# A two-layer channel network in two phases: seven block products for all four batches, hidden rows by way of DRAM

## The chip, the cores and the metric

One core of one Trainium2 chip runs the kernel. TensorE (PE) multiplies, VectorE (DVE) and ScalarE (ACT) do the elementwise work, GpSimd (POOL) and SyncE (SP) issue DMAs beside the other engines. The metric is the device time of one execution in microseconds, as the median of several.

## The reference

Four batches of 448 tokens by 768 channels go through three stages; the last is the one that changes.

```python
attn = 1 / (1 + exp(-(q @ k.T / 8 - log(448))))        # 4 batches, 12 heads, 448 x 64
x = (attn @ v), heads side by side                     # 448 x 768 per batch
k = maximum(xk @ w_k, 0); v = k * k @ w_v              # 768 -> 1024 -> 768, xk and xr mix x
x = v / (1 + exp(-(xr @ w_r)))                         # with the token before it
u = x + real(fft2(x))
un = (u - mean(u)) / sqrt(var(u) + 1e-6)               # over the 768 channels
out = u + maximum(un @ w_ch1, 0) @ w_ch2               # 768 -> 3072 -> 768
```

The weights arrive eight bytes wide and are made fp32 on the chip.

## The kernel before

A large fp32 product is made of three fp32r matmuls: both operands are split into a high part (a cast on ScalarE) and a low part (a subtraction on VectorE), and high by high, high by low and low by high are summed in PSUM. A matmul has 128 rows of weight and a moving operand of 448 columns, one batch. The helper class Order holds a planner: generators for every piece of work ask for keys (`need`), emit instructions, and its clock decides in which order each engine's queue is written. Every matmul is recorded at line 202, VectorE's two-operand work at 237 and 245, ScalarE's copies and casts at 254 and activations at 256, DMAs at 261 (POOL, accumulating) and 263. The order of a queue is fixed at build time; an instruction that must wait holds up what stands behind it on its engine.

The program runs attention, the mix (`keys`, `receptance`, `values`), and, batch by batch beside `values`, the transform: `spectrum` and `mixed` make u in `x2_t[b]` (x_0 to x_3 in the rows), `centre` and `scale` (from line 1015) subtract the mean and make rs, one over the standard deviation. In the transform, pa and qa are first-step matmuls whose split parts are called pq, and a second set of matmuls of 226 columns is recorded under pq too.

The network (`network`, line 1412) has 3072 hidden channels in 12 groups of 256. Batches 0 and 1 go through plain products: `ffn1` (36 matmuls for each 256 hidden channels and batch), `hidden` (relu and the split of h on chip), `ffn2` (36 matmuls as well), whose results `out_done` adds into `acc`, loaded from u. `convert` makes w_ch1 and w_ch2 fp32, stores them and keeps their split parts for the plain products. Batches 2 and 3, called the second pair, then go through a block form in which a 2 x 2 block product takes seven products of sums of blocks instead of eight. `PRODUCTS` lists layer one: A blocks and sums S of the weights (`second_weights` makes them, 9 matmuls a product, `pair1` with 63 a group), B blocks and sums T of the rows (`prepare_rows`, from c_d in DRAM, multiplied by rs there). `SECOND` does the same for layer two in pairs of groups (`second_weights2`, `second_rows`, `second`, `second_done`, 126 matmuls a pair of groups) for NS = 5 pairs. Each result is copied by ScalarE into a stage tile and added into DRAM by accumulating DMAs of POOL. The sixth pair of groups takes plain `ffn2` (144 matmuls), and its results with those in DRAM make the output of batches 2 and 3.

## Time and profile before

| | |
|---|---|
| median of three runs | 1159.62 us (1159.06 to 1161.45) |
| the profiled execution | 1159.6 us, its span 1157.8 us |
| TensorE busy | 1148.8 us, 99% of the span |
| VectorE, ScalarE busy | 773.2 us (67%), 602.5 us (52%) |
| DMA | 243.52 MB, 210 GB/s on average |

The time lies 1.8 us over the span, which runs from the first to the last instruction. A busy share is an average over stages; what an engine is worth in one stage is read from the windows and the timeline there. A matmul's record starts at its issue and ends when its last result is out, so records of neighbours overlap, and the distance from one start to the next (the pitch) is what a row of them costs.

### The profile page before, as it was taken

The numbers are of one execution on the slowest core, as the hardware profiler recorded it, in microseconds if no ns is written. First come the engines' busy times: TensorE is split into PE (matmuls) and PEld (weight loads), VectorE is DVE, ScalarE is ACT, GpSimd is POOL, SyncE is SP. The second block draws the span as 40 slices with busy tenths as digits, with TensorE's granted clock in tenths as the row PEclk, the third lists the DMA queues.
The fourth block names the chain that finished last, engine by engine and source line by source line (L and its number), as shares of the span: only waits on it lengthen the run. The fifth ranks groups of instructions, "written<-read, shape, count | busy, mean of one in ns | idle before, by whom it ended". The sixth has DMA issues, their size and how long they took to land.

```text
span 1157.8 us, 16560 instructions
## 1 busy us (share of the span) xinstructions
PE 1148.8 (99%) x6094; PEld 1009.1 (87%) x6094; DVE 773.2 (67%) x1293; ACT 602.5 (52%) x1091; POOL 106.7 (9%) x154
## 2 busy tenths in 40 slices
PE   8999999999999999999999999999999999999998
PEld 3576766799999999999999999999999999999998
DVE  3867757576514679898766666665477777877762
ACT  6887887667520133244544444443137567665740
POOL 0000001000000000000000000000003243442420
PEclk9999999999999999999999999999999999999999
DMA  7765789568949355476675656563917696977994
GB/s 242 241 221 210 260 311 349 227 232 290 332 141 292 109 198 192 147 283 262 212 248 193 229 196 227 199 220 112 354 40 177 126 202 110 192 136 163 181 191 167
DMA packets 92549, 243.52 MB, mean 210 GB/s; under 512 B 10610, under 2 KB 46516, under 8 KB 92340
## 3 DMA queue, kind: packets, MB, share of 16 engines
q1 hardware_dynamic: 74596, 204.70, 50.9%
q0 software_dynamic: 17584, 37.30, 17.1%
q8 instruction: 48, 0.79, 0.3%
q10 hardware_dynamic: 288, 0.46, 0.1%
q14 instruction: 33, 0.27, 0.1%
HBM read 145.45 MB, written 99.04 MB: 211 GB/s over the span
## 4 chain that ended last, share of the span: by engine, by line
PE 96%; ACT 1%; DMA 1%; DVE 0%; issue 0%; SPq 0%; DVEq 0%
PE f L202 32%; PE m L202 10%; PE v L202 10%; PE k L202 9%; PE r L202 7%; PE av L202 6%; PE sc L202 4%; PE f_W L202 4%; PE f_X L202 3%; PE f_Z L202 3%; PE f_Y L202 2%; PE pq L202 1%; DMA w<-w_d 1%; PE sc_c L202 1%; PE pa L202 1%; PE qa L202 1%
## 5 line engine op out<-in xcount | busy, mean ns | idle before, releaser
L202 PE MATMUL f<-un,w1h 128*128 128x448 f32 x576 | 164.2, 364 | 0.0
L202 PE MATMUL f<-h,w2h 128*128 128x448 f32 x576 | 163.2, 363 | 0.0
L237 DVE TENSOR_TENSOR acc<-acc,f 128x448 f32<-128x448 f32 x126 | 77.3, 618 | 79.7 <-PE f L202 79.2
L261 POOL DMA_DIRECT2D u_d<-stage x75 | 64.7, 931 | 602.9 <-ACT stage L254 595.6
L202 PEld LDWEIGHTS f<-un,w1h 128*128 128x128 f32 x576 | 108.0, 188 | 7.6 <-issue 0.6
L202 PEld LDWEIGHTS f<-h,w2h 128*128 128x128 f32 x576 | 108.1, 188 | 7.0
L202 PE MATMUL v<-k,wvh 128*128 128x448 f32 x384 | 111.9, 365 | 0.0
L202 PE MATMUL f<-un,w1l 128*128 128x448 f32 x288 | 103.9, 361 | 0.0
L202 PE MATMUL f<-h,w2l 128*128 128x448 f32 x288 | 103.7, 360 | 0.0
L202 PE MATMUL m<-hs,sw_h 128*128 128x448 f32 x324 | 91.5, 363 | 0.0
L256 ACT ACTIVATE sg<-sc,bias_s 128x448 f32<-128x448 f32 x144 | 78.3, 650 | 12.9 <-PE sc L202 12.8
L202 PEld LDWEIGHTS v<-k,wvh 128*128 128x128 f32 x384 | 72.0, 188 | 4.9 <-issue 0.6
L202 PE MATMUL k<-xkh,wkh 128*128 128x448 f32 x192 | 70.6, 368 | 0.9 <-ACT kt L256 0.9
L202 PE MATMUL k<-xkl,wkh 128*128 128x448 f32 x192 | 70.2, 366 | 0.0
L202 PE MATMUL k<-xkh,wkl 128*128 128x448 f32 x192 | 70.2, 366 | 0.0
L202 PE MATMUL v<-k,wvl 128*128 128x448 f32 x192 | 69.7, 363 | 0.0
L254 ACT COPY stage<-m 128x448 f32<-128x448 f32 x105 | 55.7, 534 | 16.8 <-PE m L202 7.0
L202 PEld LDWEIGHTS m<-hs,sw_h 128*128 128x128 f32 x324 | 60.8, 188 | 4.0
L256 ACT ACTIVATE h<-f 128x448 fp32r<-128x448 f32 x48 | 26.1, 544 | 71.3 <-PE f L202 71.3
L202 PE MATMUL m<-hs,sw_l 128*128 128x448 f32 x162 | 58.3, 360 | 0.0
L202 PEld LDWEIGHTS f<-un,w1l 128*128 128x128 f32 x288 | 53.9, 187 | 3.9 <-issue 0.2
L202 PE MATMUL av<-sg,v 128*64 128x448 f32 x288 | 57.2, 544 | 0.0
(227 smaller groups left out, 2502.1 us busy)
## 6 DMA issues: line engine op xcount, KB each, us to landing
w_raw<-in_w SPq DMA_DIRECT2D x40, 768.0 KB, 4.8
u_d<-stage POOLq DMA_DIRECT2D x75, 224.0 KB, 5.9
w_d<-w_bits SPq DMA_DIRECT2D x40, 384.0 KB, 2.6
k_d<-kp SPq DMA_DIRECT2D x32, 448.0 KB, 3.2
k<-k_d SPq DMA_DIRECT2D x32, 448.0 KB, 5.9
a<-w_d SPq DMA_DIRECT2D x24, 384.0 KB, 5.4
w<-w_d SPq DMA_DIRECT2D x24, 384.0 KB, 10.6
v<-in_v SPq DMA_DIRECT2D x24, 256.0 KB, 3.5
```

The costliest lines, as they stand in the source:

```text
L202: self.nc.tensor.matmul(out, lhs, rhs, start=start, stop=stop, skip_group_check=skip)
L237: eng.tensor_tensor(out, a, c, op=op)
L254: self.nc.scalar.copy(out, a)
L256: self.nc.scalar.activation(out, a, fn, **kw)
L261: self.nc.gpsimd.dma_start(out, src, accum_op=ALU.add)
```

## The change

All four batches go through the block form, as pair 0 (batches 0 and 1) and pair 1 (2 and 3), and the network has two phases.

In phase one only layer one runs. The first PL = 4 groups of pair 0 are still plain (8 chunks of 128 hidden channels, `plain`, 18 matmuls a chunk and batch). Then come 15 visits: groups 4 to 6 for pair 0, groups 7 to 11 for both pairs with the same weight sums, and groups 0 to 6 for pair 1. A visit is 63 matmuls a pair. The seven products are ordered anew and use three PSUM banks a pair; a copy of the first product, the seed, starts the second bank chain. The relu results go to DRAM unsplit (`put`, h_d). `rows0` and `rows1` make the operands of the pairs; the rows of pair 1 stay on chip and are worked on 1344 wide, and the results of batches 1 to 3 need no way through c_d. w_ch2 is converted in halves in phase one (`convert_rest`), its seven pieces and sums (`combine`) go to DRAM (v_d).

In phase two `second` takes one pair after the other: seven products, each over six steps (`tp`) of two groups and 18 matmuls. A product's 36 matmuls for one result are summed in one PSUM bank, three results beside each other; products 0 and 2, 1 and 3, 4 and 6 share a chain. `second_splits` loads the weight piece (w, 768 wide) and the hidden rows (r, 896 wide) of a step, subtracts rows where a T is asked for, and splits both (sw, hs). Results are added on VectorE into tiles loaded from u and stored to the output; no accumulating DMA is left. `convert` for the plain products, `ffn2`, `master`, `second_done` and the way of rs through DRAM are gone; their lines are left out below.

```diff
+PL, JO, EARLY = 4, 7, 8
...
 PRODUCTS = (
     ("A11", "B11", "X"),
+    ("S3", "T3", "W"),
     ("S2", "T2", "Y"),
-    ("S3", "T3", "Z"),
+    ("A12", "B21", "X"),
+    ("S1", "T1", "Y"),
+    ("A22", "T4", "W"),
+    ("S4", "B22", "Y"),
+)
+SECOND = (
+    ("A11", "B11", "X"),
     ("S1", "T1", "W"),
     ("A12", "B21", "X"),
+    ("S4", "B22", "W"),
+    ("S3", "T3", "Z"),
+    ("S2", "T2", "Y"),
     ("A22", "T4", "Z"),
-    ("S4", "B22", "W"),
 )
-LATE = ("T1", "B21", "T4", "B22")
-SECOND = (("A11", "B11"), ("S1", "T1"), ("A12", "B21"), ("S4", "B22"), ("S2", "T2"), ("S3", "T3"), ("A22", "T4"))
-NS = NG // 2 - 1
+PIECE = {nm: i for i, (nm, _, _) in enumerate(SECOND)}
+VISITS = [(g, (0,)) for g in range(PL, JO)] + [(g, (0, 1)) for g in range(JO, NG)] + [(g, (1,)) for g in range(JO)]
+LAST0 = 7 * (NG - PL) - 1
+CHUNKS = FF2 // 128
...
-            if b > 1:
-                o.at["c_d", b, i] = o.dma(c_d[b][:, 2 * i : 2 * i + 2], xx) + 2.0
             if b > 0 and i == 0:
-        if b > 1:
-            yield from o.need(("c_d", b, 2))
-            o.at["centre", b] = o.now
-            yield from scale(b)
-            return
         yield from scale(b)
         rs = rs_t[b]
         for i in range(KD):
             t = o.tt(V, u[:, i], u[:, i], rs, ALU.mult)
             yield t
-            if i % 2:
+            o.at["norm", b, i] = t
+            if i % 2 and b < 1:
                 o.at["c_d", b, i // 2] = o.dma(c_d[b][:, i - 1 : i + 1], u[:, i - 1 : i + 1]) + 2.0
-        yield from o.need(("c_d", b, 2))
+        if b < 1:
+            yield from o.need(("c_d", b, 2))
         o.at["centre", b] = o.now
...
+        yield from o.need(("centre", 2))
+        yield from split("B11", *new("B11"), b11)
+        yield from split("B21", *new("B21"), b21)
+        yield from o.need(("centre", 3), ("rows", 0))
+        v = x2_t[3]
+        b12, b22 = v[:, 0:3], v[:, 3:6]
+        o.dma(t_d[1], b22)
+        yield o.tt(V, b11, b12, b11, ALU.subtract)
+        t1 = np_.tile([128, 2, 3, S], F32R, tag="x2", name="T1_1", bufs=3)
+        yield from split("T1", t1[:, 0], t1[:, 1], b11)
+        yield o.tt(V, b12, b22, b12, ALU.subtract)
+        yield from split("T3", *new("T3"), b12)
+        yield o.tt(V, b12, b22, b11, ALU.subtract)
+        yield from split("T2", *new("T2"), b12)
+        yield o.tt(V, b21, b21, b12, ALU.subtract)
+        yield o.dma(t_d[0], b21) + 2.0
+        for i, nm in enumerate(("T4", "B22")):
+            t = np_.tile([128, 2, 3, S], F32R, tag="x2", name=f"{nm}_1", bufs=3)
+            yield o.dma(t[:, 1].bitcast(F32), t_d[i]) + 0.5
+            yield from split(nm, t[:, 0], t[:, 1], t[:, 1].bitcast(F32))
+        shift(tp1, "tp1")
+        o.at["rows", 1] = o.now
+    wt_t, place_t = {}, {}
+    for v, (g, ps) in enumerate(VISITS):
+        for j in range(2):
+            i = 2 * (v - NG + PL) + j
+            place_t[v, j] = ("w0", "w1", "k0", "k1", "k2")[i % 5] if i >= 0 else f"w{j}"
+    def visit_loads():
+        last = {}
+        for v, (g, _) in enumerate(VISITS):
...
+        def visit(v):
+            g, ps = VISITS[v]
+            bk, tm = {}, {}
+            def after(n, p):
+                x, y, w = (bk[k, p][:, 0:S] if (k, p) in bk else None for k in "XYW")
+                    bk["Y", p] = bank(f"f1_{v}_{p}_Y")
+                    o.at["seed", v, p] = o.act(bk["Y", p][:, 0:S], x)
+                    o.at["w7", v, p] = o.act(tmp("w7", p), w)
+                    o.at["u2", v, p] = o.act(tmp("u2", p), y)
+                    yield from put(p, 0, g, stage(p, 0, g), x)
+                    o.at["c22", v, p] = t = o.tt(V, tm["w7", p], tm["w7", p], y, ALU.add)
+                    yield t
+                    yield from put(p, 3, g, tm["w7", p], tm["w7", p])
+                    yield o.tt(V, tm["u2", p], tm["u2", p], w, ALU.add)
+                    yield from put(p, 2, g, tm["u2", p], tm["u2", p])
+                    yield from put(p, 1, g, stage(p, 1, g), y)
...
+            def step(n, p, i, lhs, rhs, k):
+                if i == 0 and n < 2:
+                    bk[k, p] = bank2(f"f1_{v}_{p}_{k}")
+                o.mm(bk[k, p][:, 0:S], lhs, rhs, i == 0 and n < 2, i == 8, skip=True)
...
-        order = [(ffn1, "w1", (0, 0)), (ffn1, "w1", (1, 0)), (ffn2, "w2", (0, 0))]
-        order += [(ffn1, "w1", (0, 1)), (ffn1, "w1", (1, 1)), (ffn2, "w2", (0, 1)), (ffn2, "w2", (1, 0))]
-        order += [(ffn1, "w1", (2, 0)), (ffn2, "w2", (1, 1)), (ffn1, "w1", (2, 1))]
-        for g in range(2, NG, 2):
-            order += [(ffn1, "w1", (g, 0)), (ffn1, "w1", (g, 1))] if g > 2 else []
-            order += [(ffn2, "w2", (g, 0))]
-            order += [(ffn1, "w1", (g + 1, 0)), (ffn1, "w1", (g + 1, 1)), (ffn2, "w2", (g + 1, 0)), (ffn2, "w2", (g + 1, 1))]
-        order += [(pair1, "p1", (0, 3)), (pair1, "p1", (1, 3))]
-        for p in range(NS):
-            order += [(second, "s2", (p, range(5))), (pair1, "p1", (2 * p + 2, 3))]
-            order += [(second, "s2", (p, (5, 6))), (pair1, "p1", (2 * p + 3, 3))]
-        order += [(ffn2, "v2", (NG - 1, 2)), (ffn2, "v2", (NG - 1, 3))]
...
+        def second(p):
+            def after(m, e, ps):
...
+                if m == 0:
+                    if e == 0:
+                        tiles("t")
+                    o.at["tc", p, e] = o.act(out[p, "t"][:, e], ps)
+                elif m == 1:
+                    if e == 0:
+                        tiles("22", "11")
+                    yield from o.need(("res", p, "22"))
+                    o.at["v", p, e] = add("22", e, ps)
+                elif m == 2:
+                    yield from store("11", e, add("11", e, ps))
+                elif m == 3:
+                    if e == 0:
+                        tiles("12", "21")
+                    yield from o.need(("res", p, "12"))
+                    o.at["w", p, e] = add("12", e, ps)
+                elif m == 4:
+                    o.at["z", p, e] = add("22", e, ps)
+                elif m == 5:
+                    t = out[p, "t"][:, e]
+                    yield o.tt(V, t, t, ps, ALU.add)
+                    t1, t2 = add("12", e, t), add("22", e, t)
+                    o.at["y", p, e] = add("21", e, t)
+                    yield from store("12", e, t1)
+                    yield from store("22", e, t2)
+                else:
+                    yield from store("21", e, add("21", e, ps))
+                yield o.now
+            def step(m, e, i, j, lhs, rhs):
+                first = {2: 0, 3: 1, 6: 4}.get(m, m)
+                if i == 0 and first == m:
+                    chain[p, m, e] = (bank2 if m in (0, 4) else bank)(f"m_{p}_{m}_{e}")
+                ps = chain[p, first, e][:, 0:S]
+                o.mm(ps, lhs, rhs, i == 0 and first == m, i == 35, skip=True)
+                if i == 35:
...
+            for m in range(7):
+                for tp in range(NG // 2):
+                    j = 42 * p + 6 * m + tp
+                    for t in range(2):
+                        for e in range(3):
+                            es = slice(128 * e, 128 * e + 128)
+                            for i, (a, c) in enumerate(((0, 0), (0, 1), (1, 0))):
+                                o.feed.append(partial(step, m, e, 6 * tp + 3 * t + i, j, sw[:, a, t, es], hs[:, c, t]))
...
+        for b in range(2):
+            pss = ([], [])
+            for t in (0, 3):
+                for f in range(2):
+                    yield from plain(f, b, range(t, t + 3), pss[f])
+        for f in range(2, 2 * PL):
+            for b in range(2):
+                yield from plain(f, b)
+        for v in range(len(VISITS)):
+            yield from visit(v)
+        for p in range(2):
+            yield from second(p)
...
+        for j in range(total):
+            p, m, tp = j // 42, j % 42 // 6, j % 6
+            if j > 1:
+                yield from o.need("right")
+            if j > 3:
+                yield from o.need(("pair", j - 4))
+            w, t = raw.pop(j)
+            yield t
+            sw_t[j] = from_pool(j, "sw", [128, 2, 2, n], F32R, f"sw_{j}")
+            yield o.act(sw_t[j][:, 0], w)
+            o.spawn(low(("sw", j), sw_t[j], w))
+            nm = SECOND[m][1]
+            q = {"B11": (0,), "T1": (1, 0), "B21": (2,), "B22": (3,), "T3": (3, 1), "T2": (3, 0), "T4": (2, 3)}[nm]
+            for x in q:
+            r = [r_t[p, x, tp] for x in q]
+            dst = r[{"T1": 1, "T3": 1}.get(nm, 0)]
+            if len(q) > 1:
+                yield o.tt(V, dst, r[0], r[1], ALU.subtract)
+            hs_t[j] = from_pool(j, "hs", [128, 2, 2, S], F32R, f"hs_{j}")
+            yield o.act(hs_t[j][:, 0], dst)
+            o.spawn(low(("hs", j), hs_t[j], dst))
...
+        if (f % 2, h) == (1, 1):
+            store("A22", w)
+            pc["S1"] = piece(f"s1_{g}")
+            yield from combine("S1", pc["S1"], pc[0, 1], w, ALU.add)
+        elif (f % 2, h) == (0, 0):
+            store("A11", w)
+            pc["S2"] = piece(f"s2_{g}")
+            yield from combine("S2", pc["S2"], pc["S1"], w, ALU.subtract)
+            yield from combine("S3", pc[0, 1], w, pc[0, 1], ALU.subtract)
+        elif (f % 2, h) == (1, 0):
+            store("A12", w)
+            yield from combine("S4", piece(f"s4_{g}"), w, pc["S2"], ALU.subtract)
...
+        yield from convert(wst, "raw", 3, 3, todo1, room, ready)
+        yield from o.need(("rows", 1))
+        yield from convert(wst, "raw", 3, 3, todo2, room, ready, None, 3.5)
+        yield o.now + 4.0
+        o.at["converted"] = o.now
```

By count, layer one and two together have 3258 matmuls of 448 columns before and 3060 now.

The first place is VectorE in the transform of batch 3, between the addition that ends block 3 of x_3 and the low parts of qa. xl and yl are low parts of the transform's operands, evod, xf and yf its folded rows, h the hidden part of a plain product. Before:

```order
L237 TENSOR_TENSOR xl_5288<-xf_5278,xh_5287 128x2x225
L245 SCALAR_TENSOR_TENSOR h_0_0_5354<-f_0_0_0_5313,h_0_0_5354 128x448
L237 TENSOR_TENSOR yl_5290<-yf_5279,yh_5289 128x2x223
L237 TENSOR_TENSOR evod_5189<-x_3_4853 128x448 x2
L237 TENSOR_TENSOR xf_5278<-evod_5189 128x223
L895 COPY xf_5278<-evod_5189 128x2
L237 TENSOR_TENSOR yf_5279<-evod_5189 128x223
L237 TENSOR_TENSOR x_2_4377<-x_2_4377,mean_5365 128x448 x2
L245 SCALAR_TENSOR_TENSOR h_0_1_5393<-f_0_0_1_5351,h_0_1_5393 128x448
L237 TENSOR_TENSOR xl_5288<-xf_5278,xh_5287 128x225
L237 TENSOR_TENSOR xf_5278<-evod_5189 1x223
L904 COPY xf_5278<-evod_5189 1x2
```

Now, with un_1 the low parts of batch 1's normalized rows, x_1 times rs their source, and s and blk the first weight sums of the visits:

```order
L248 TENSOR_TENSOR sum_u_5373<-sum_u_5373,x_2_4477 128x448 x2
L248 TENSOR_TENSOR x_3_4986<-v_5_5379,rv_5_5326 128x448
L248 TENSOR_TENSOR x_1_4072<-x_1_4072,rs_5259 128x448
L248 TENSOR_TENSOR un_1_5473<-x_1_4072,un_1_5473 128x448
L248 TENSOR_TENSOR xl_5427<-xf_5417,xh_5426 128x2x225
L248 TENSOR_TENSOR yl_5429<-yf_5418,yh_5428 128x2x223
L248 TENSOR_TENSOR sum_u_5373<-sum_u_5373,x_2_4477 128x448 x2
L248 TENSOR_TENSOR s_0_5506<-a_1_5469 128x384
L248 TENSOR_TENSOR blk_5507<-a_0_5465,blk_5507 128x384
L248 TENSOR_TENSOR evod_5358<-x_3_4986 128x448 x2
L248 TENSOR_TENSOR xf_5417<-evod_5358 128x223
L915 COPY xf_5417<-evod_5358 128x2
```

The two hidden parts have gone, and the scaling and the low parts of un_1, sums of x_2 and weight sums have come between the same folds.

The second place is VectorE where the rows of pair 1 are made. Before, acc_6321 is the tile in which four 448-wide row blocks are combined, among the sums and splits of plain products for batch 0:

```order
L237 TENSOR_TENSOR acc_5367<-acc_5367,f_6_0_2_7123 128x448
L237 TENSOR_TENSOR acc_6321<-acc_6321 128x448
L237 TENSOR_TENSOR acc_5367<-acc_5367,f_6_0_3_7132 128x448
L237 TENSOR_TENSOR w2l_1_7048<-w_7_1_bits,w2h_1_7047 128x768
L237 TENSOR_TENSOR acc_5367<-acc_5367,f_6_0_4_7147 128x448
L237 TENSOR_TENSOR T_1_7160<-acc_6321,T_1_7160 128x448
L237 TENSOR_TENSOR acc_5367<-acc_5367,f_6_0_5_7156 128x448
```

Now this is the start of the visits, from a sum of visit 0 (w_0) to the low part of the second product of visit 1 (blk_6407):

```order
L248 TENSOR_TENSOR w_0_6294<-w_0_6294,f_0_0_Y 128x448
L248 TENSOR_TENSOR T_1_6352<-x_2_4477,T_1_6352 128x1344
L248 TENSOR_TENSOR u_0_6318<-u_0_6318,f_0_0_W 128x448
L248 TENSOR_TENSOR s_1_6358<-a_1_6315 128x384
L248 TENSOR_TENSOR blk_6359<-a_0_6290,blk_6359 128x384
L256 SCALAR_TENSOR_TENSOR w_23_1_6363<-w_23_raw_6298,w_23_1_6363 128x384
L248 TENSOR_TENSOR x_3_4986<-x_3_4986 128x1344
L248 TENSOR_TENSOR a_1_6315<-a_0_6290,a_1_6315 128x384
L248 TENSOR_TENSOR T_1_6405<-x_3_4986,T_1_6405 128x1344
L248 TENSOR_TENSOR a_0_6290<-s_1_6358,a_0_6290 128x384
L248 TENSOR_TENSOR blk_6407<-a_1_6315,blk_6407 128x384
```

A row operation is now three blocks wide, and three such instructions stand ahead of a low part of the very next product.

The third place is VectorE in layer two. Before, in the middle of a pair of groups:

```order
L237 TENSOR_TENSOR a_1_9362<-a_0_9360,a_1_9362 128x384
L237 TENSOR_TENSOR hs_0_9421<-rows,hs_0_9421 128x448
L237 TENSOR_TENSOR a_0_9360<-s_5_9400,a_0_9360 128x384
L237 TENSOR_TENSOR hs_1_9422<-rows,hs_1_9422 128x448
L237 TENSOR_TENSOR sw_l<-w_2_9249,sw_h 128x768
L237 TENSOR_TENSOR rows<-rows 128x896
L237 TENSOR_TENSOR blk_9418<-a_0_9360,blk_9418 128x384
```

Now, in the last product of pair 0 (T4, a difference of rows):

```order
L248 TENSOR_TENSOR r_3_2_9057<-r_3_2_9057,r_0_2_8066 128x896
L248 TENSOR_TENSOR sw_9764<-w_9675,sw_9764 128x768
L248 TENSOR_TENSOR out_0_9272<-out_0_9272,m_4_0_9627 128x448
L248 TENSOR_TENSOR out_0_9272<-out_0_9272,m_4_1_9631 128x448
L248 TENSOR_TENSOR out_0_9272<-out_0_9272,m_4_2_9635 128x448
L248 TENSOR_TENSOR hs_9782<-r_3_2_9057,hs_9782 128x896
L248 TENSOR_TENSOR r_3_3_9069<-r_3_3_9069,r_0_3_8911 128x896
L248 TENSOR_TENSOR sw_9797<-w_9703,sw_9797 128x768
```

The weight sums (blk, a, s) of layer one have left this place; a step now has one subtraction of rows, one low part of weights and one of rows, and the three sums of a finished product stand between them.

## Rows read from the trace of the kernel before

**Rows 1.** The page, busy time and share of the span by engine

```profile
PE 1148.8 (99%) x6094; PEld 1009.1 (87%) x6094; DVE 773.2 (67%) x1293; ACT 602.5 (52%) x1091; POOL 106.7 (9%) x154
```

**Rows 2.** The span and TensorE's mean granted clock, by core

```profile
core 0: 1157.8 us, clock 1.000
```

**Rows 3.** Waits of TensorE: what it waited for, us in all, times, longest

```profile
PE sc L202 <- DMA q<-in_q: 3.8, 1, 3.8
PE k L202 <- ACT kt L256: 0.9, 3, 0.5
PE f_W L202 <- DVE u L237: 0.4, 1, 0.4
```

**Rows 4.** Groups by line and shape, TensorE: busy us, mean ns of one

```profile
L202 PE MATMUL f<-un,w1h 128*128 128x448 f32 x576 | 164.2, 364 | 0.0
...
L202 PE MATMUL m<-hs,sw_h 128*128 128x448 f32 x324 | 91.5, 363 | 0.0
```

**Rows 5.** Timeline, TensorE in layer two: start, us, operation, count

```profile
719.70 0.36 PE L202 MATMUL f<-h,w2l 128*128 128x448 f32 x1
...
720.30 0.36 PE L202 MATMUL f<-h,w2l 128*128 128x448 f32 x1
...
723.90 0.36 PE L202 MATMUL f<-h,w2l 128*128 128x448 f32 x1
```

**Rows 6.** Timeline, VectorE: back to back instructions of four widths

```profile
905.11 0.55 DVE L237 TENSOR_TENSOR s<-a 128x384 f32<-128x384 f32 x1
905.58 0.62 DVE L237 TENSOR_TENSOR extra<-rows,extra 128x448 fp32r<-128x448 f32 x1
906.12 0.55 DVE L237 TENSOR_TENSOR a<-a,a 128x384 f32<-128x384 f32 x1
...
908.46 1.09 DVE L237 TENSOR_TENSOR rows<-rows 128x896 f32<-128x896 f32 x1
909.46 0.95 DVE L237 TENSOR_TENSOR w<-w 128x768 f32<-128x768 f32 x1
910.33 0.55 DVE L237 TENSOR_TENSOR blk<-a,blk 128x384 fp32r<-128x384 f32 x1
```

**Rows 7.** Timeline, VectorE in the transform of batch 3

```profile
484.13 0.62 DVE L237 TENSOR_TENSOR x<-v,rv 128x448 f32<-128x448 f32 x1
...
508.98 0.56 DVE L237 TENSOR_TENSOR pq<-qa,pq 111x384 fp32r<-111x384 f32 x1 [0.60 <-ACT pq L254]
```

**Rows 8.** Busy time of each engine in that stretch

```profile
487.40:509.00 21.60, 21.60 (x132) 20.10 (x131) 19.71 (x44) 8.93 (x18) 0.00 (x0) 1.00 0.95 346
```

**Rows 9.** Timeline, ScalarE: casts and a copy of three widths

```profile
879.53 0.84 ACT L254 CAST sw_h<-w 128x768 fp32r<-128x768 f32 x1
880.27 0.54 ACT L254 COPY stage<-m 128x448 f32<-128x448 f32 x1
880.69 0.53 ACT L254 CAST blk<-a 128x384 fp32r<-128x384 f32 x1
```

**Rows 10.** DMA of the fullest 20 us of the network

```profile
DMA packets 2893, 7.31 MB, mean 365 GB/s; under 512 B 325, under 2 KB 1318, under 8 KB 2892
```

**Rows 11.** The page, DMA issues: count, KB each, us to landing

```profile
w_raw<-in_w SPq DMA_DIRECT2D x40, 768.0 KB, 4.8
u_d<-stage POOLq DMA_DIRECT2D x75, 224.0 KB, 5.9
...
a<-w_d SPq DMA_DIRECT2D x24, 384.0 KB, 5.4
```

**Rows 12.** Timeline, the end of the span

```profile
1152.26 2.73 SPq L263 DMA_DIRECT2D out<-acc  x2
...
1153.61 0.36 PE L202 MATMUL f<-h,v_l 128*128 128x448 f32 x1
1154.01 0.62 DVE L237 TENSOR_TENSOR acc<-acc,f 128x448 f32<-128x448 f32 x1 [1.78 <-PE f L202]
```

**Rows 13.** Busy time and granted clock just after the first wait

```profile
3.80:8.00 4.20, 4.16 (x16) 1.88 (x19) 0.17 (x1) 1.93 (x4) 0.00 (x0) 1.00 0.94 272
```

836 lines of the change are left out of this document (394 added, 442 removed).

## The prediction

> **What bounds the kernel now.** I read the page first, then the clock, TensorE's waits, its groups, and only then single stretches. TensorE is busy for 1148.8 of 1157.8 us [rows 1] at a granted clock of 1.000 [rows 2], and its waits come to 5.1 us, of which 3.8 are the first load [rows 3]. VectorE is busy for 67% and ScalarE for 52% [rows 1]; nobody waits for them. So the time now is the list of matmuls times their pitch, and every matmul less is time gained, as long as the helpers stay hidden. The second question is therefore how near each helper is to showing, stretch by stretch.
>
> The duration of one matmul, 363 or 364 ns [rows 4], is not its price, since matmuls overlap. In the timeline 21 of them start between 719.70 and 723.90 [rows 5]: 4.20 / 21 = 0.200 us. The same holds for VectorE: one 448-wide sum lasts 0.62 us, but the next starts 0.54 behind it; 384 wide 0.47, 896 wide 1.00, 768 wide 0.87 [rows 6]. From 448 to 896 is 0.46 more, so 1344 wide is 1.46 by the same slope. On ScalarE a 768 cast is 0.74, a 448 copy 0.42 [rows 9].
>
> **What is removed.** Before, layer one of batches 0 and 1 is 2 x 24 x 18 = 864 matmuls and their layer two another 864; batches 2 and 3 take 12 x 63 = 756 and 5 x 126 = 630, and 144 for their last group pair: 3258. After: 2 x 8 x 18 = 288 plain ones, 20 block products of a pair and group, 20 x 63 = 1260, and 2 x 42 x 18 = 1512: 3060. All have 448 columns, and the rest of TensorE's list is the same. 198 x 0.200 = **39.6 us less**. The 0.4 us wait of f_W for u [rows 3] goes with its pattern. The 75 accumulating stores of 224 KB [rows 11] go too, at nothing: TensorE never waited for them. If every new step hid as well, the time would be 1159.6 - 39.6 - 0.4 = 1119.6. The profiled execution took 1159.6 with a span of 1157.8, and the median of the runs is 1159.62, so no correction is due.
>
> **What is added, and where it shows.** I went along VectorE's queue between two points at which it meets TensorE, summed pitches, and set that against TensorE's work between the same points.
>
> (a) The transform of batch 3. From x of column block 3 to the second pq low part VectorE has 49 instructions before, whose pitches sum to 22.2 us; they took from 484.13 to 509.54, 25.4 us [rows 7]. In 21.6 us of this it was busy for 19.71 while TensorE never paused [rows 8]: already over nine tenths full, 1.9 us of waiting, and 23.5 / 22.2 = 1.06 times the pitches for dependent and PSUM operands. After, the same stretch holds 88: 45 of 448 wide (24.1), 24 of about 224 at 0.30 by the slope (7.2), 9 of 384 or 390 (4.2), 7 of about 448 (3.8) and three tiny ones, 39.5 us. The new ones are the scaling of x_1, the low parts of un_1 and T_0, and the work on x_2, which used to stand later or went by way of DRAM. TensorE has 129 full matmuls (25.8 us), 83 of 192 to 226 columns (7.7 in proportion) and one of the mean, some 35 us. With 0.4 us from a last matmul to VectorE's start [rows 12]: 39.5 x 1.06 + 0.4 - 35 = 7.3. The ends are 4.9 (bare pitches) and 10.4 (1.14, the 25.4 with its waits). VectorE is the late one here, so ScalarE's waits mostly vanish: I take **7.3**.
>
> By the Trainium skill (VectorE: DVE Perf Modes, section "The TRN2 errata — SBUF-src ops pay a fixed extra latency per instruction") an fp32 sum costs (N + 151) / 0.96 ns, 0.624 us for 448, and the fixed part is exposed between instructions. The trace agrees with it for one instruction, 0.62, and not for a row of them, 0.54 [rows 6]. By the page the stretch would be an estimated 47 us and this term 12.
>
> (b) The rows of pair 1. Between the sum of visit 0's fifth product and the low part that visit 1's second product needs, VectorE now has three 1344-wide instructions (4.4), a 448 sum and seven of 384 (3.3), 8.3 us with the first sum, where TensorE has 29 matmuls, 5.8. Before, the same rows came one 448 block at a time, with ffn products around them. 8.3 + 0.4 - 5.8 = 2.9; the third 1344 instruction also waits for a cast of some 1.2 us on ScalarE (by the slope of [rows 9]), of which 0.5 is covered: **3.7**, ends 2 and 5.
>
> (c) The visits of pair 1 alone. One is 63 matmuls, 12.6 us. In the four densest SP issues some 21.8 MB (weights twice 384 KB per visit, halves of w_ch2 in, seven pieces out, hidden rows out, first rows of layer two in): 21.8 MB / 50.4 us = 430 GB/s, where the fullest 20 us of the trace moved 365 [rows 10]. 21.8 MB at 365 is 59.7 us: the queue falls 9 us behind and later catches up. Three raw buffers and five weight places take up about half. A late raw half is worse than its own delay: ScalarE meets it in order, and the casts and seed copies behind it are what TensorE waits for. I take **4**, ends 0 and 12.
>
> (d) The start of layer two: its first weight load is issued at the phase's end, lands in some 3 to 5 us (5.4 for 384 KB [rows 11]), and then a cast of 0.74 and a low part of 0.87 [rows 6, 9] stand before TensorE, which has two pairs made up ahead, 7.2 us: **1**, ends 0 and 2.
>
> (e) Layer two. A step of 18 matmuls is 3.6 us; VectorE needs 0.87 + 1.00, and one sum of 1.00 more where the row operand is a difference, 2.87, four of seven products. During the last product of a pair six such steps and the twelve sums of the product before come to 17.2 + 6.5 = 23.7 us, with two casts' waits perhaps 25, against 21.6, with three steps made up ahead (10.8): **1** in all, ends 0 and 3. Accumulating six groups in PSUM takes the eviction copies out of the middle, and nothing replaces them on TensorE.
>
> (f) The end: three results 0.6 us apart instead of two [rows 12]: **0.5**.
>
> Together 7.3 + 3.7 + 4 + 1 + 1 + 0.5 = 17.5, and 1119.6 + 17.5 = **1137** us. The ends sum to 7 and 33.
>
> **The rivals.** *Everything hides*: the planner's order is only an order, and a late VectorE might be caught up by un tiles that were ready earlier. Then 1120 to 1130. For it speaks that before shows no wait with VectorE 91% full [rows 8]; against it that (a) and (b) are sums in one queue, with no other way round. *DMA holds phase one's second half*: (c) at its 430 GB/s not absorbed at all and repeated in the visits that stand beside it, 10 to 18 us instead of 4, so 1143 to 1155. *Conversion gates layer two*, the slower side: 48 halves of w_ch2 stand between the rows of pair 1 and the phase's end, about 1080 matmuls or 216 us, 4.5 us per half. The last pieces are needed five steps, 18 us, into layer two, plus 10 left before it. If a half takes over 5.1 us it shows; at 5.6, 48 x 1.1 = 53 us late less 28 gives 25 on top of 17.5, and slower than before begins there, at about 1162. For it: ScalarE and VectorE take them in order with all else. Against: a half is 0.7 MB in and out, 2 us at 365 GB/s, and about 1.8 us on either engine. *The clock falls*: where TensorE waits in (a) it is granted 1.2 instead of 2.4 GHz, 35 us of work lasts 70 and the stretch gains some 27 us: 1164. The row against it is the first stretch, granted 1.00 right behind 3.8 us without a matmul [rows 3, 13]. The Trainium skill (TensorE: Matmul & The Clock Gate, "HAM oscillation — how this bites in real kernels") tells of kernels whose waits between short bursts lower the clock again and again; this trace shows no such fall. *The count doesn't fall* is out: the built program has 198 matmuls less.
>
> **How the numbers follow.** The forecast, 1131 to 1143, has 0.50; everything hides 0.17; DMA 0.22; conversion 0.04; the clock 0.02; 0.05 lies between the DMA case and no change or beyond. A measurement tells apart about 0.2%, 2.3 us: faster is below 1157.3, same up to 1161.9. Faster is 0.50 + 0.17 + 0.22 + 0.02 = 0.91, same 0.03, slower 0.06. For 8 in 10 the range runs from 1122, the upper part of the hidden case, to 1154.
>
> **What would show it.** In the changed kernel: 198 matmuls less at a pitch of 0.200; TensorE waits for VectorE's un and pq of about 7 us in all around the transform of batch 3; a wait for blk of 3 to 4 at the second visit; waits for blk or seed copies with raw halves behind them in the last seven visits; little in layer two. It is wrong if layer two's steps wait for hs or sw all along, if the granted clock shows anything under 1.00, or if the pitch of a chain of 36 matmuls differs from 0.200.

## The result and the profile after

The changed kernel takes **1148.94 us** (median of four runs, 1146.42 to 1152.25) where the kernel before took 1159.66 beside it: a ratio of 0.9907 with a 95% interval of 0.9878 to 0.9936. That is 10.7 us less, faster as forecast and inside the range, but under half of the 22.6 us that the forecast of 1137 promised. The profiled execution took 1147.87 us with a span of 1146.1.

The page of the changed kernel, busy time by engine and what the DMA moved:

```profile
PE 1119.5 (98%) x5896; PEld 974.3 (85%) x5896; DVE 804.6 (70%) x1295; ACT 646.7 (56%) x1158; POOL 16.1 (1%) x49
...
DMA packets 116021, 278.87 MB, mean 243 GB/s; under 512 B 13216, under 2 KB 58464, under 8 KB 115808
```

Against [rows 1] the 198 matmuls have gone: 6094 to 5896. TensorE idles for 1146.1 - 1119.5 = 26.6 us where it idled for 9.0, so 17.6 us of idle time came in, almost the 17.5 of the forecast's sum. The surprise stands in the same row: busy time fell only from 1148.8 to 1119.5, by 29.3 us and not by 39.6. Some 10 us of TensorE's time went where no wait is counted.

TensorE's mean granted clock, which was 1.000 [rows 2]:

```profile
core 0: 1146.1 us, clock 0.995
```

TensorE's waits in the changed kernel (us in all, times, longest), against [rows 3]:

```profile
PE f_Y L213 <- ACT u L265: 3.8, 1, 3.8
PE sc L213 <- DMA q<-in_q: 3.7, 1, 3.7
PE var L213 <- ACT sq L265: 2.5, 1, 2.5
PE f_W L213 <- ACT blk L265: 2.2, 1, 2.2
PE f L213 <- DVE un L248: 2.2, 1, 2.2
PE f L213 <- DVE x L248: 1.8, 1, 1.8
PE f_W L213 <- DVE blk L248: 1.4, 1, 1.4
PE m L213 <- DVE hs L248: 1.1, 2, 0.7
```

The first seven are one event each, of 1.4 to 3.8 us, and not a toll in every visit. Behind the wait for `var`, behind the two at visit 1 and at the end of the longest, the clock falls. Busy time and granted clock in the stretch of the fall and in an equally long one behind it (stretch; its length and the busy us and instructions of PE, PEld, DVE, ACT, POOL; the granted clock; DMA share; GB/s):

```profile
427.52:430.93 3.41, 3.41 (x17) 3.27 (x16) 0.50 (x3) 1.45 (x4) 0.00 (x0) 0.50 0.64 184
430.94:434.35 3.41, 3.41 (x32) 3.29 (x31) 3.34 (x7) 2.18 (x5) 0.00 (x0) 1.00 0.04 8
...
591.36:594.77 3.41, 3.41 (x11) 3.05 (x10) 3.38 (x6) 2.15 (x3) 0.00 (x0) 0.50 0.00 0
594.78:598.19 3.41, 3.41 (x19) 3.18 (x18) 2.96 (x4) 1.49 (x3) 0.00 (x0) 1.00 0.76 205
...
765.44:768.85 3.41, 2.94 (x8) 2.64 (x9) 2.94 (x5) 3.41 (x7) 0.00 (x0) 0.50 1.04 379
768.86:772.27 3.41, 3.41 (x19) 3.19 (x18) 2.89 (x5) 1.70 (x4) 0.00 (x0) 1.00 1.05 395
```

The granted clock is 0.50, the 1.2 GHz level, for 3.41 us each time. TensorE counts as busy, but about half as many matmuls run in the stretch: 17 against 32 (of several widths), 11 against 19 and 8 against 19 (all of 448 columns). A fall costs half of what TensorE works in it: 1.7 us for each of the first two, and 1.5 for the third, whose first 0.47 us are still a wait. Three cost 4.9, all of it inside busy time.

Place by place, in distances from start to start less the pitch of 0.200 (the waits in brackets in a timeline are about 0.16 shorter, since the record of the matmul before covers that much):

| place | forecast | profiled execution |
|---|---|---|
| (a) transform of batch 3 | 7.3 | 5.7 (1.98 + 2.68 + 1.02) |
| `var`, 422 to 427 us | none | 3.5 (2.66 + 0.82) |
| (b) rows of pair 1 at visit 1 | 3.7 | 4.0 (2.41 + 1.61) |
| (c) visits of pair 1 alone | 4 | 4.6 (0.63 + 3.99) |
| (d) start of layer two | 1 | 1.35 (0.42 + 0.93) |
| (e) layer two | 1 | 0.6 |
| (f) the end | 0.5 | 0 |
| the clock | none | 4.9 (three falls) |
| all smaller gaps | none | 3.6 |
| sum | 17.5 | 28.3 |

1119.6 + 28.3 is 1147.9, the profiled execution. The row of smaller gaps is what was left over; 0.8 of it are two waits of `v` for loads from k_d at 376 us. Of the 10 us for which no wait is counted, 4.9 are the falls; the rest is the 0.16 us of each wait that a record covers, and gaps shorter than a record.

**The wait that was not in the forecast**, at `var`. The timeline of the changed kernel there (start, us, engine, operation; in brackets the idle time before it and what ended it):

```profile
422.51 0.37 PE L213 MATMUL v<-k,wvl 128*128 128x448 f32 x1
422.85 0.62 DVE L248 TENSOR_TENSOR x<-v,rv 128x448 f32<-128x448 f32 x1 [4.92 <-DMA rv<-r_d]
...
424.75 0.56 ACT L265 CAST sq<-sum_v 128x448 fp32r<-128x448 f32 x1 [6.20 <-DVE sum_v L248]
...
425.37 0.47 PE L213 MATMUL var<-sq,one 128*128 128x448 f32 x1 [2.50 <-ACT sq L265]
```

VectorE stands for 4.92 us before an instruction that needs rv, the receptance rows of `values` on their way back from DRAM; the sums of squares stand behind it in its queue, and TensorE's `var` behind those. In the 13 us before, the DMA engines were full:

```profile
410.00:423.00 13.00, 12.87 (x65) 11.72 (x63) 7.41 (x16) 4.24 (x8) 0.00 (x0) 1.00 1.00 371
```

In the kernel before, the same 13 us moved 238 GB/s at a share of 0.66:

```profile
410.00:423.00 13.00, 13.00 (x82) 12.26 (x81) 10.56 (x24) 6.17 (x11) 0.00 (x0) 1.00 0.66 238
```

Now w_ch1 is converted there: raw halves in, fp32 halves out, on the SP queue in which the rv loads stand too. From 404 to 414.9 us that queue held eight loads of k before as well, but two raw halves and a store of the conversion have come between them, and all eight loads of k now stand ahead of rv. SP issued the two rv loads at 410.51 and 412.58 us before, and at 414.91 and 415.78 now; the first took 6.0 us to land before and takes 7.8 now.

**The wait in the visits of pair 1.** The timeline of the changed kernel, ScalarE and two DMA issues of SP at 757 us:

```profile
757.07 0.32 SPq L274 DMA_DIRECT2D h_d<-w  x1
...
759.15 0.32 SPq L274 DMA_DIRECT2D h_d<-u  x1
...
763.93 0.53 ACT L265 COPY w<-f_W 128x448 f32<-128x448 f32 x1 [5.37 <-DMA h_d<-w]
...
765.32 0.53 ACT L265 COPY u<-f_Y 128x448 f32<-128x448 f32 x1
```

ScalarE may copy this visit's W chain into its tile w7 only once the store of the last visit's w7, issued at 757.07, has read it; it stands 5.37 us for it, and the copy u, for which TensorE's next product waits, comes behind it. The DMA engines are full there (750.00 to 775.00: share 1.02, 392 GB/s).

### The profile page after: what moved, and what is told of

Read it like the earlier page. It is cut to its first block, busy times and chain, and to the rows that moved or that the text cites. A ratio compares the mean times of both kernels' runs of the same rounds, so it can differ in the third digit from the quotient of the medians.

```text
span 1146.1 us, 16758 instructions
## 1 busy us (share of the span) xinstructions
PE 1119.5 (98%) x5896; PEld 974.3 (85%) x5896; DVE 804.6 (70%) x1295; ACT 646.7 (56%) x1158; POOL 16.1 (1%) x49
## 4 chain that ended last, share of the span: by engine, by line
PE 87%; DMA 5%; DVE 4%; ACT 2%; issue 1%; SPq 0%; ACTq 0%; DVEq 0%
PE m L213 24%; PE k L213 9%; PE f_Y L213 8%; PE v L213 8%; PE r L213 8%; PE av L213 6%; PE f_W L213 6%; PE f_X L213 5%; PE sc L213 4%; PE f L213 4%; PE pq L213 1%; DMA k<-k_d 1%; DMA a<-w_d 1%; PE sc_c L213 1%; PE pa L213 1%; DVE out L248 1%
## 5 line engine op out<-in xcount | busy, mean ns | idle before, releaser
L213 PE MATMUL m<-hs,sw 128*128 128x448 f32 x1512 | 304.0, 362 | 1.5 <-DVE hs L248 1.1
L213 PEld LDWEIGHTS m<-hs,sw 128*128 128x128 f32 x1512 | 283.2, 188 | 22.1 <-DVE hs L248 2.3
L265 ACT CAST sw<-w 128x768 fp32r<-128x768 f32 x84 | 70.0, 833 | 90.4 <-PE m L213 50.8
L265 ACT CAST hs<-r 128x896 fp32r<-128x896 f32 x84 | 78.9, 940 | 65.4 <-DVE r L248 65.4
L248 DVE TENSOR_TENSOR sw<-w,sw 128x768 fp32r<-128x768 f32 x84 | 80.2, 954 | 50.3 <-ACT sw L265 50.1
L248 DVE TENSOR_TENSOR hs<-r,hs 128x896 fp32r<-128x896 f32 x84 | 91.3, 1087 | 8.6 <-ACT hs L265 8.6
L213 PE MATMUL f_Y<-T,blk 128*128 128x448 f32 x360 | 79.7, 371 | 3.8 <-ACT u L265 3.8
L213 PE MATMUL f_W<-T,blk 128*128 128x448 f32 x360 | 78.4, 365 | 3.8 <-ACT blk L265 2.2
L213 PEld LDWEIGHTS f_Y<-T,blk 128*128 128x128 f32 x360 | 69.4, 194 | 9.6 <-ACT u L265 4.2
L213 PE MATMUL f<-un,w1h 128*128 128x448 f32 x192 | 56.2, 368 | 4.0 <-DVE un L248 2.2
```

What stands on the lines that cost most here:

```text
L213: self.nc.tensor.matmul(out, lhs, rhs, start=start, stop=stop, skip_group_check=skip)
L248: eng.tensor_tensor(out, a, c, op=op)
L265: self.nc.scalar.copy(out, a)
```

## The experiments

All were timed in three rounds beside the kernel before (1160.2 to 1160.3 in these); "after" is the changed kernel.

**1. rv on another queue.** The question is whether the wait at `var` comes from rv's place behind the conversion's transfers in SP's queue, or from the full DMA engines, which would delay rv on any queue; and whether the fall behind it goes with the wait.

```diff
-                o.dma(t, r_d[b][e])
+                o.dma(t, r_d[b][e], G)
```

> One word changed in the changed kernel: the loads of rv, the receptance rows that a finished column block of the values is multiplied by, are issued by POOL instead of SP, so that they no longer stand behind four loads of k of 448 KB in SP's queue. In the changed kernel rv took about 8 us to land, VectorE stood 4.9 us before it, and TensorE waited 2.50 and 0.55 us for the variance, with the granted clock at 0.50 for 3.4 us right behind. Theory A (the clock falls behind a wait): the two waits go and the stretch at 0.50 goes with them, so 3.1 + 1.7 = about 4.8 us less, near 1144 against 1148.9. Theory B (the clock falls whatever the waits): the waits go, a stretch at 0.50 stays somewhere, about 3 us less. Theory C (the DMA engines are full, whoever issues): rv lands as late as before and nothing changes.

Measured: 1142.87 us (1142.29 to 1143.89), ratio 0.9849 [0.9834, 0.9864], 6.1 us under after. Windows of this kernel:

```profile
418.00:427.50 9.50, 9.50 (x63) 8.98 (x62) 6.79 (x15) 6.06 (x13) 1.09 (x2) 1.00 0.86 340
427.52:430.93 3.41, 3.41 (x29) 3.26 (x29) 3.24 (x7) 2.05 (x5) 0.00 (x0) 1.00 0.45 118
```

TensorE is never idle in 418 to 427.5, and the fall behind it is gone; the other two falls stay. 3.5 for the wait, 1.7 for the fall and 0.8 for the k_d loads make 6.0. The issue of the same load by SP in the changed kernel, and then by POOL here, with the instruction of VectorE that needs it:

```profile
414.91 1.19 SPq L274 DMA_DIRECT2D rv<-r_d  x2
```

```profile
411.39 0.55 POOL L274 DMA_DIRECT2D rv<-r_d  x1 [8.05 <-DVE x L248]
...
418.27 0.62 DVE L248 TENSOR_TENSOR x<-v,rv 128x448 f32<-128x448 f32 x1 [0.83 <-DMA rv<-r_d]
```

It was the place in the queue: POOL issues the load 3.5 us earlier. With the DMA engines still at a share of 0.86 it takes 6.8 us to land instead of 7.8, and VectorE waits 0.83 us for it instead of 4.92.

**2. The rows of pair 1 in thirds.** The 1344-wide work of `rows1` in 448-wide steps that the planner may spread, 0.5 us apart.

```diff
+LAG = 0.5
...
-            yield o.act(hi, src)
-            t = o.sub(V, lo, src, hi)
             for d in range(3):
+                yield o.act(hi[:, d], src[:, d])
+                t = o.sub(V, lo[:, d], src[:, d], hi[:, d])
...
-                yield t + LAG
```

> The rows of pair 1 are made 448 wide, three instructions where the changed kernel has one of 1344, with a short pause of the planner between them; the work is the same. In the changed kernel TensorE waited 2.24 and 1.45 us at the second product of visit 1, with the granted clock at 0.50 for 3.4 us behind it. By the sum of the queue VectorE now has 5.4 us of work against 5.8 there, so these waits go. Theory A (the clock falls behind a wait): 3.7 + 1.7 = about 5.4 us less, near 1143.5. Theory B (clock falls whatever the waits): 3.7 less. Rival: 20 more instructions on VectorE move the wait to a later visit: no change.

Measured: 1151.55 us (1150.86 to 1151.63), ratio 0.9921 [0.9905, 0.9938]. Both waits at visit 1 are gone, so the wide instructions caused them. But 3.2 us come back at 630 to 637 us, where the rows now reach a later visit late, more at 754 and 845, and there are five falls instead of three. The gain went into new waits.

**3. A slower pace for layer two's first rows.** If their loads filled the DMA engines in the last visits, spacing them out should take the wait at 762 us away.

```diff
-                yield o.now + (6.0 if odd is False else 2.0)
+                yield o.now + (9.0 if odd is False else 2.0)
```

> The first rows of layer two (r, 448 KB each) are loaded every 9 us instead of every 6 us in the visits of pair 1 alone. In the changed kernel the DMA moved 392 GB/s there, a store of a visit's hidden rows took 6.9 us, ScalarE stood 5.4 us for it, and TensorE waited 3.83 us, with the clock at 0.50 behind. If the fullness of the DMA at this place is the cause, the wait goes down by 2 to 4 us and with it 1.7 of the clock: 2 to 5.5 us less, 1143.5 to 1147. If it is the order of SP's queue (the store stands behind loads whatever their pace) the wait stays: no change.

Measured: 1148.35 us (1146.74 to 1149.83), ratio 0.9895 [0.9878, 0.9912], not told apart from after. The wait went from 3.99 to 3.07, and two smaller ones appeared at 814 and 849 us (0.62 and 0.94). The profiled execution also has a fall of 6.83 us behind `var`, twice as long as in after. These loads are not the main cause of the wait.

**4. Weight sums and rows of pair 0 later.** To lighten VectorE around the transform of batch 3, both generators wait for its end.

```diff
         yield from o.need(("centre", 1))
+        yield from o.need(("four", B - 1))
...
+        yield from o.need(("four", B - 1))
         for v in range(len(VISITS)):
```

> The first weight sums and the T rows of pair 0 are begun only after the transform of batch 3, instead of inside it. That takes some 5 weight sums and low parts and the first T rows (about 6 us by pitches) out of VectorE's queue ahead of the low parts of un_1 and pq of batch 3, where TensorE waited 1.81, 2.17 and 0.87 us in the changed kernel. If VectorE's load in this stretch is the cause, as the prediction's term (a) had it, the later two waits shrink: 1.5 to 3 us less there. If the same work then comes late at the first visit, a wait of about that size appears there and the time stays.

Measured: 1153.07 us (1149.21 to 1154.30), ratio 0.9930 [0.9908, 0.9953]. The second wait of (a) went from 2.68 to 1.75, but the visits now start behind: 3.14, 1.28 and 3.70 us at 573 to 579, and falls of 6.83, 6.83 and 3.41 us. The work was moved, not removed, and where it went it was late by more.

**5. The hidden rows' stores on POOL's queue**, on top of 1.

```diff
-        o.at["h", p, q, g] = o.dma(h_d[p][q][g // 2][:, g % 2], dst) + 2.0
+        o.at["h", p, q, g] = o.dma(h_d[p][q][g // 2][:, g % 2], dst, G) + 2.0
```

> On top of the first experiment (rv loaded by POOL; 1142.9): the stores of the hidden rows of layer one go out by POOL too instead of SP. At the first visits of pair 1 alone, ScalarE stood 5.4 us for such a store, which was issued on SP behind weight and row loads and took 6.9 us, and TensorE waited 3.5 us in the first experiment, with 3.4 us at half clock behind it. If the queue's order is the cause (a store behind loads of SP), the wait goes: 3.5 + 1.7 = 5.2 less, near 1137.7. If the 16 engines' fullness is the cause, the store takes as long by any queue: no change.

Measured: 1142.57 us (1141.75 to 1146.30), ratio 0.9858 [0.9839, 0.9877], the same as 1. The wait for u shrinks from 3.3 to 2.6, and ScalarE still stands for the store:

```profile
757.05 0.53 ACT L265 COPY w<-f_W 128x448 f32<-128x448 f32 x1 [3.79 <-DMA h_d<-w]
```

Here the queue is not the main cause, unlike in 1: the store takes 5.8 us to land where it took 6.8 by SP, with the DMA engines as full (share 1.02 in both), and the tile is single.

**6, 7, 8. Work from VectorE to POOL.** Number 6 moves the four 1344-wide subtractions of `rows1` (on top of 1), 7 does that on top of 5, and 8 moves the scaling of x_1 as well.

```diff
-        yield o.tt(V, b11, b12, b11, ALU.subtract)
+        yield o.tt(G, b11, b12, b11, ALU.subtract)
```

> On top of the first experiment: the four 1344-wide subtractions of the rows of pair 1 are made by POOL instead of VectorE. They took 4 x 1.46 us of VectorE around visits 0 and 1, where TensorE waited 2.2 and 1.5 us. Splitting them by three moved the wait to the visit that needs the rows; taking them off VectorE should not, if VectorE's sum is the cause: 3.7 + 1.7 = 5.4 less, near 1137.5. If POOL slows VectorE down while it works, or the rows then come too late for the fourth visit, the wait comes back there: 0 to 2 less.

> Both of the former on top of the first. Theory A (each wait costs itself and a stretch at half clock): the two gains add up, 5.2 + 5.4 less, near 1132, and the granted clock is 1.00 but for the start. Theory B (stretches at half clock come whatever the waits): 7.2 less, near 1135.7.

```diff
-            t = o.tt(V, u[:, i], u[:, i], rs, ALU.mult)
+            t = o.tt(G if b == 1 else V, u[:, i], u[:, i], rs, ALU.mult)
```

> On top of both: the six multiplications of x_1 by rs (batch 1) are made by POOL instead of VectorE, in the stretch where TensorE waited 1.8, 2.2 and 0.9 us for un_1 and x of batch 3. That takes 6 x 0.54 = 3.2 us out of VectorE's queue there, and the planner draws some T rows into it. If VectorE's sum is the cause, as term (a) of the prediction had it, 2 to 4 us of the 5 go; if the T rows take the room, or POOL's own pace (not shown by any row so far) sets un_1, the waits stay.

Measured: 1147.20 us (1145.48 to 1147.66), ratio 0.9884 [0.9869, 0.9899]; 1153.08 (1150.79 to 1155.85), 0.9939 [0.9921, 0.9956]; 1157.42 (1155.90 to 1159.21), 0.9974 [0.9964, 0.9983]. Each is slower than the kernel that it builds on, by 4.3, 10.5 and 4.3 us. The timelines of POOL and VectorE in kernel 6 show what happened there:

```profile
568.73 3.30 POOL L248 TENSOR_TENSOR x<-x 128x1344 f32<-128x1344 f32 x1 [2.62 <-DVE x L248]
587.29 6.71 POOL L248 TENSOR_TENSOR x<-x,x 128x1344 f32<-128x1344 f32 x2 [15.26 <-DVE T L248]
```

```profile
568.99 3.46 DVE L256 SCALAR_TENSOR_TENSOR w<-w_raw,w 128x384 uint32<-128x384 uint32 x1
572.37 0.61 DVE L248 TENSOR_TENSOR T<-x,T 128x448 fp32r<-128x448 f32 x1
...
588.40 2.65 DVE L248 TENSOR_TENSOR blk<-s,blk 128x384 fp32r<-128x384 f32 x1 [0.73 <-ACT blk L265]
590.98 0.61 DVE L248 TENSOR_TENSOR w<-w,f_Y 128x448 f32<-128x448 f32 x1
591.51 0.61 DVE L248 TENSOR_TENSOR u<-u,f_W 128x448 f32<-128x448 f32 x1
593.44 1.97 DVE L248 TENSOR_TENSOR T<-x,T 128x1344 fp32r<-128x1344 f32 x1 [1.32 <-ACT T L265]
```

POOL needs 3.3 us for what VectorE does in 1.55, and a 384-wide instruction of VectorE that otherwise lasts 0.55 lasts 3.46 and 2.65 beside it: begun while POOL works (568.73 to 572.03, and 587.29 to about 590.6), it ends some 0.4 us behind POOL's. The two sums at 590.98 and 591.51, with one operand in PSUM (f_Y, f_W), run beside POOL's second instruction at their usual 0.61. So VectorE gained nothing while POOL worked, and the rows came later by POOL's slowness. The Trainium skill (SBUF — State Buffer, "Who interferes with whom") says that a VectorE instruction with two SBUF inputs contends with a GpSimd instruction that reads SBUF, since its second input comes through the read interface that both share, and it calls the contention an exclusive lock; these rows agree.

In 7 the instructions held (3.49 us from 580.98 and 3.78 from 599.55) make weight sums and low parts that TensorE needs next, and it waits 3.73 and 4.22 us. In 8 the six multiplications take POOL 7.94 us from 479.86, and TensorE's wait for x in (a) grows from 1.9 to 5.95 us.

**9. Two places mended**, on top of 5: the rows of pair 1 in thirds without a pause (`split` likewise, as in 2), and two tiles by turns for w7 and u2 in the visits of pair 1 alone.

```diff
+        def three(out, a, c):
+            for d in range(3):
+                yield o.tt(V, out[:, d], a[:, d], c[:, d], ALU.subtract)
...
-        yield o.tt(V, b11, b12, b11, ALU.subtract)
+        yield from three(b11, b12, b11)
...
-                if p == 0:
+                if p == 0 or v >= NG - PL and v % 2 == 0:
```

> On top of rv and the hidden rows' stores by POOL's queue (1142.6): the rows of pair 1 in thirds without the planner's pause (they then end at about the place in VectorE's queue where they did before the split), and the two intermediate sums of a visit (w7, u2) in two buffers by turns in the visits of pair 1 alone, so that ScalarE need not wait there for the last visit's store. Place 1, visit 1: TensorE waited 2.24 and 1.44 us with 3.4 us at half clock behind; if the 1344-wide blocks at the head of VectorE's queue are the cause, the waits go and don't come back at the fourth visit (they did with the pause). Place 2, the first visit of pair 1 alone: it waited 2.63 us; if the single buffer behind a full DMA is the cause, that wait goes. Both gone: 6.3 + 3.4 = 9.7 less, near 1133. One gone: 1137 to 1138. If the full DMA shows through another load at place 2, a wait stays there under another name.

Measured: **1134.91 us** (1134.39 to 1135.27), ratio 0.9778 [0.9763, 0.9792]: the fastest of all, 14.0 us under after and 25.4 under the kernel before. The page, the clock and two windows of it:

```profile
PE 1114.9 (98%) x5896; PEld 970.4 (86%) x5896; DVE 806.6 (71%) x1317; ACT 648.1 (57%) x1172; POOL 81.1 (7%) x169
```

```profile
core 0: 1133.5 us, clock 1.000
```

```profile
575.00:600.00 25.00, 23.66 (x114) 20.62 (x113) 22.86 (x44) 17.33 (x37) 3.79 (x7) 1.00 0.46 166
...
750.00:775.00 25.00, 24.39 (x120) 21.85 (x119) 20.07 (x39) 19.06 (x41) 4.32 (x8) 1.00 1.04 409
```

At visit 1 the wait is 0.82 instead of 2.41 and 1.61, with another of 0.85 behind it 14 us on; the wait for u is gone although the DMA engines are as full as before, and no fall is left in the execution. What the second tile did shows in the timeline of POOL and ScalarE:

```profile
747.61 0.55 POOL L274 DMA_DIRECT2D h_d<-w  x1 [6.63 <-issue]
...
751.39 0.52 ACT L265 COPY w<-f_W 128x448 f32<-128x448 f32 x1
```

The store of the last visit's w7 still takes 5.9 us to land, until 753.5, but ScalarE's copy for this visit begins at 751.39. Against 5 the waits fell by 2.35 at visit 1 and by 1.84 in the visits of pair 1 alone (3.83 to 1.99), and two falls are 3.3: 7.4, where the medians differ by 7.7 and the profiled executions by 6.5.

**10, 11. A wait made on purpose**, in layer two, where kernel 5 has none: one cast of hidden rows is repeated (same result), 13 or 17 times, on top of 5.

```diff
-            yield o.act(hs_t[j][:, 0], dst)
+            for _ in range(13 if j == 60 else 1):
+                t = o.act(hs_t[j][:, 0], dst)
+            yield t
```

> A wait made on purpose in layer two, where the kernel of the fifth experiment (1142.6) has neither a wait nor a fall of the clock: one cast of rows in the middle of pair 1's layer two is done 13 times over (0.86 us each), with the result unchanged. TensorE has about 8 us of steps made up ahead, so it should wait 2 to 3 us there. Theory A (the clock falls behind a wait of this size): a stretch of 3.4 us at a granted 0.50 follows, in some runs or all, and the time grows by the wait or the wait and 1.7. Theory B (the clock falls for other reasons): no stretch at 0.50 there, the time grows by the wait alone.

> The same with 17 casts: a wait of 5 to 6.5 us. Theory A: a stretch at a granted 0.50 follows in every run, and the time grows by the wait and 1.7 us (3.4 us at half clock); it does not grow with the wait's length. Theory B: the time grows by the wait alone.

Measured: 1149.03 us (1148.06 to 1150.26), ratio 0.9900 [0.9885, 0.9915], and 1151.84 (1149.90 to 1154.39), 0.9926 [0.9907, 0.9946]: 6.5 and 9.3 us over 5. Windows of kernel 10, the wait, the fall and the stretch behind it, and then of kernel 11:

```profile
1051.60:1055.90 4.30, 1.03 (x5) 0.37 (x4) 2.36 (x4) 4.21 (x6) 0.00 (x0) 1.00 0.43 160
1055.97:1059.38 3.41, 3.41 (x10) 3.03 (x11) 3.41 (x4) 3.36 (x5) 0.00 (x0) 0.50 0.38 115
1059.39:1062.80 3.41, 3.41 (x18) 3.19 (x18) 2.79 (x4) 1.68 (x2) 0.00 (x0) 1.00 0.66 202
```

```profile
1049.00:1053.40 4.40, 0.64 (x4) 0.26 (x2) 1.30 (x3) 4.24 (x6) 0.00 (x0) 1.00 0.43 156
1053.51:1060.34 6.83, 3.82 (x9) 3.06 (x10) 4.22 (x5) 6.77 (x9) 0.00 (x0) 0.50 0.16 46
1060.35:1067.18 6.83, 6.83 (x35) 6.39 (x35) 4.75 (x6) 3.33 (x5) 0.00 (x0) 1.00 0.63 184
```

In kernel 10 TensorE starts 2.78 and 0.93 us late, 3.7 together, and 1.7 of the fall follow: 5.4 of the profiled execution's 8.5 over 5's. The rest lies elsewhere, in places that the edit does not touch: 1.7 at 376 us, 1.1 at visit 1, where the fall lasts 6.83 us instead of 3.41, and 0.9 in the visits of pair 1 alone. In kernel 11 TensorE starts 6.66 and 0.93 late; the clock falls inside the wait, for 6.83 us, of which the last 4.2 lie behind the wait, and the slow matmuls there cost 1.5: 9.1 in all, where the profiled executions differ by 9.8 and the medians by 9.3. Here nothing but a wait was added, in a stretch that had no fall, and a fall came with it, once in each profiled execution: so the wait is its cause, and not full DMA engines (share 0.43) or a busy VectorE.

## Where the prediction was right, and the step that failed

**Right**: the 198 matmuls and their pitch. In 900.00 to 925.00 the changed kernel starts 125 matmuls, 0.200 us each. Experiment 9 shows the base of the forecast with the clock at 1.000: its gaps after the first 300 us come to 18.2 where before has 3.5, and 1119.6 + 14.8 = 1134.4 is its time within 1 us.

**Right by place and nearly by size**: (a) 5.7 for 7.3, (b) 4.0 for 3.7, (d), (e), (f) within half a microsecond each. Experiments 2 and 9 showed for (b) that it was the wide instructions; its text counts seven 384-wide ones where the queue has six, and its 8.3 us fit six. In (a) VectorE is as full as the forecast had it:

```profile
484.00:506.00 22.00, 20.19 (x112) 18.74 (x111) 21.66 (x49) 6.97 (x14) 0.00 (x0) 1.00 0.47 152
```

Against [rows 8] it is busy for 21.66 of 22.0 us, and now TensorE waits. The size is nearer to the bare sum of pitches than I took it: the lower end was 4.9, and 4.7 came from VectorE, with 1.0 more for a load of w1l that the term did not have. That VectorE's full queue is the cause in (a) is read from these rows; no experiment took the waits away. 4 lowered the second from 2.68 to 1.75, and 8 made the first longer.

**Right size, other mechanism**: (c). The forecast saw late raw halves in front of ScalarE. What held ScalarE was the store of its own last result from a single tile; 3 and 5 left the wait in being, and it went in 9, whose second tile let the copy start ahead of the store's landing, at the same DMA share. (In 7 and 8 it all but went without a second tile, behind an earlier wait of 1.7 to 1.8 us for weight sums, in which the store could land.) That the DMA engines would be full there, 392 against 365 GB/s [rows 10], was right, but that alone did not cost 10 to 18 us, as the second rival had it.

**Missed**: the load of rv, 3.5 us. The sum went along VectorE's queue in (a) and the DMA load in (c), and not along SP's queue in between. There the loads of k and the transfers of the w_ch1 conversion now stand ahead of rv, on which VectorE, ScalarE and `var` hang one behind the other; experiment 1 took the wait away. That the conversion is what filled the DMA engines is read from the traces; no run left it out.

**The step that failed**: the clock. The sum has no term for it: the forecast counted each wait at its length alone. As a rival the clock had a chance of 0.02 and was priced as all of (a) at half speed, 27 us; the evidence against it was [rows 13], a granted clock of 1.00 right behind the first wait. In the changed kernel three falls cost 4.9 us; without them the profiled execution would have taken 1143.0, the upper end of the forecast. The prediction had named a granted clock under 1.00 as a sign of being wrong. The row that it set against this rival was no reading. In the changed kernel the same column for the time before any matmul, and the first products:

```profile
0.00:3.70 3.70, 0.00 (x0) 0.00 (x0) 0.06 (x1) 1.49 (x2) 0.33 (x6) 1.00 0.41 138
...
7.70:11.90 4.20, 4.20 (x28) 1.64 (x28) 0.00 (x0) 4.20 (x10) 0.00 (x0) 1.00 0.97 336
```

```profile
3.74 4.46 PE L213 MATMUL sc<-q,k 64*128 64x448 f32 x12 [3.74 <-DMA q<-in_q]
...
9.04 2.53 PE L213 MATMUL sc<-q,k 64*128 64x448 f32 x12
```

The column gives 1.00 for a stretch in which TensorE did nothing, since the record of the clock begins later, at 7.68 us (7.17 in the kernel before); and the same twelve products took 4.46 us there and 2.53 later. The kernel before shows it in the very row that I quoted: 16 matmuls in 4.20 us, where its next 4.20 us hold 28:

```profile
8.00:12.20 4.20, 4.20 (x28) 1.75 (x28) 0.00 (x0) 4.20 (x9) 0.00 (x0) 1.00 1.00 355
```

Read by its count, that row would have spoken for the rival. The price was wrong in form too: a fall here lasts 3.41 us and costs 1.5 to 1.7, once behind each of three waits, and not a whole stretch. The Trainium skill (TensorE: Matmul & The Clock Gate, "HAM oscillation — how this bites in real kernels") tells of it, for short bursts between DMA waits, as a fall for each wait whose price is half of the time throttled. The prediction quoted the Trainium skill there and set the row above it; on the price the trace of the changed kernel agrees with the Trainium skill (11 matmuls where the next 3.41 us count 19).

So of the 10.8 us between the profiled execution and the forecast 4.9 are falls, 3.5 the wait for rv, 3.6 smaller gaps, and the forecast's own terms were 1.3 too high. The spread of the changed kernel's runs fits: 1146.42, 1147.87, 1150.02 and 1152.25 us came at mean clocks of 0.996, 0.995, 0.992 and 0.991, and experiment 9's four, three at 1.000 and one at 0.999, lie within 0.9 us.

**What stays open**: which waits bring a fall. Taken as the brackets show them, every wait of 2.5 us or more behind the first load had a fall within 3 us of its end or in itself, and so had the pair of 2.24 and 1.45 at visit 1. The wait of 1.8 to 1.9 us for x in (a) was followed by none in after and in seven of the experiments, but by one in 2, 6 and 10, at the same place and of the same length. Elsewhere falls came behind waits of 1.3 to 1.6 us (1.51 in 2, 1.39 in 6, 1.34 in 8), and none came behind the 2.17 us for un in (a), in after and in six experiments, or behind 2.04 us for u in 6. The length is open as well: falls lasted 6.83 us in 3, 4, 7, 8, 10 and 11, at 1.5 to 2.9 us each, and the fall behind `var` did so in 3 and 4 where it lasted 3.41 in after and 2. The 3.6 us of smaller gaps were not traced either.
